# Attention pairs and sequence mixing on one core: another order of Q and K preparation, score groups, mixing steps and first loads

## The chip, the cores and the metric

The kernel runs on one NeuronCore of one Trainium2 chip. The metric is the time on the device for one execution, in microseconds (us), as the median of several runs. The engines are TensorE (PE for matmuls, PEld for its weight loads), VectorE (DVE), ScalarE (ACT), GpSimd (POOL) and SyncE (SP), which here only issues transfers.

## The reference

Three blocks follow one another: windowed attention, a block that mixes along the sequence and then through a wide layer (here called sequence mixing and the wide layer), and a gated layer at the end.

```python
# attention: B=2, H=8, S=768, D=64, n_global=8, n_local=96
scores = scale * np.matmul(q, k.transpose(0, 1, 3, 2))
keep = is_global | is_local               # rel >= 0 and rel < n_local, or column < n_global
scores = np.where(keep, scores + bias[None], -1000000000.0)
a = softmax(scores)                       # written out with max, exp and sum
x = np.matmul(a, v)                       # then heads are put side by side: (2, 768, 512)
# sequence mixing and wide layer
h = x.transpose(0, 2, 1) @ U @ V          # rank 32, along the sequence
u = x + h.transpose(0, 2, 1)
x = u + np.maximum(u @ w_ch1, 0.0) @ w_ch2    # 512 -> 2048 -> 512
# gated layer
xk = mu_k * x + (1.0 - mu_k) * x_prev;  xr = mu_r * x + (1.0 - mu_r) * x_prev
k = np.maximum(xk @ w_k, 0.0)
out = sigmoid(xr @ w_r) * (k * k @ w_v)
```

## The kernel before

The weight matrices come as 64-bit floats. The kernel loads their bits, turns them into 32-bit floats by integer and float operations (`conv`: names `stg`, `cvt`, `cvc`) and splits each into a high and a low part, so that a dense product is three matmuls.

**Attention** works on eight pairs of heads. Heads 2p and 2p+1 of one batch lie on partitions 0 to 63 and 64 to 127. Each pair is one call of `slot(pp)`, which emits four kinds of work: for the current pair the scores in three groups of two blocks of 128 rows (`score(pp, 0)`, `2`, `4`) and the division by the row sums (`norm`); for the next pair the transposes and copies of Q and K (`qprep`, `kprep`); for the pair before the transposes of the probabilities P (`trans`, six groups) and the product with V (`pv`); and the loads for pairs ahead (`load_qk(pp + 2)`, `load_v(pp)`).

In a score group TensorE writes two PSUM banks, VectorE adds the distances and reduces (line 301), ScalarE takes the exponential with a running sum (line 304), and GpSimd multiplies P by the inverse sums (line 315). `qprep` is six transposes on TensorE (line 261) and two copies on ScalarE (line 263); `kprep` is the same with lines 277 and 280, and then GpSimd copies K's first 32 columns beside each block (line 282). `trans` copies its bank to SBUF through `ecopy`, every third time on ScalarE (line 472), else on VectorE (line 474).

PSUM has eight banks in two rings of four: `"a"` for scores and the dense layers' first products, `"t"` for all transposes, for `pv`, for the mixing and for the dense layers' second products. A tile of a ring waits until the tile four places back has been read. P has ten buffers; q and k as loaded have one buffer each, v two.

**Side work** is woven into the slots by `weave`, which spreads the steps of several lists evenly: weight conversions (`CONV`), and from slot 5 on the sequence mixing of batch 0 (`u_steps(0)`, sixteen steps: six transposes `xtp`, the matmuls `gps` with U, the step `gs` that makes `uv` through ScalarE and VectorE, and eight matmuls `hps` with V with an addition to `yp` on VectorE, line 530), its split into high and low parts (`u_split`, lines 551 and 552, to `us`) and the first matmuls of the wide layer (`m_ch1`, `aps`). After the last slot the same mixing follows for batch 1 with `m_ch2` (`bps`, added to `yp` in line 592) between its steps. Then come the rest of the wide layer and the gated layer, dense matmuls to the end.

**Order.** The program text emits the steps; a planner of the framework then sets the order of each engine's queue, with the order of emission as priority and a plan of when buffers come free. Each engine runs its queue in order. So an instruction can run earlier than its place in the text: the two first loads of q for pair 1 are emitted before the loads of v for pair 0 and issued after most of them.

At the start `load_qk(0, "q")`, `limits()` (two loads on ScalarE's queue, three operations on VectorE), a few idle matmuls (`warm`) and `load_qk(0, "k")` are emitted first, then `qprep(0)`, `windows()` (the table of distances), `kprep(0)`, `load_qk(1)` and `load_v(0)`.

## Time and profile before

| what | value |
|---|---|
| median of 3 runs | 572.84 us |
| the three runs | 572.84, 572.85, 568.08 us |
| the profiled execution | 567.52 us |
| its span in the profile | 565.7 us |
| mean granted clock of TensorE | 0.985 |
| TensorE busy | 537.9 us, 95% of the span |

The profile is of one execution. Its span runs from the first instruction to the last; the time of the execution is a little longer. A busy share of TensorE is not a share of its peak, since matmuls overlap and their ends are modelled. The granted clock is a share of 2.4 GHz; the lower of its two levels is 1.2 GHz.

### The profile page before, as it was taken

The page shows a single profiled execution, that of the slowest core. Times are in us where ns is not written, and L with a number is a line of the kernel's source. Part 1 is how long each engine was busy: PE and PEld are TensorE (multiplying, and loading weights), DVE is VectorE, ACT ScalarE, POOL GpSimd, SP SyncE. Part 2 cuts the span into 40 slices and gives each one's busy share as a digit, 9 for nine tenths or more (in the row PEclk, how much of TensorE's full clock was granted, in tenths as well). Part 3 has the DMA queues.
Part 4 walks back from the last instruction along what each step waited for, and adds up shares of the span by engine and source line. Part 5 has one row for each costly group of instructions (what it writes and reads, how often), then busy time and mean ns, then how long its engine had stood idle before and what let it go on. Part 6 is the DMA issues. An engine that isn't in the chain of part 4 may idle for free.

```text
span 565.7 us, 7722 instructions
## 1 busy us (share of the span) xinstructions
PE 537.9 (95%) x2814; PEld 435.2 (77%) x2814; DVE 324.4 (57%) x703; ACT 230.4 (41%) x525; POOL 182.9 (32%) x223
## 2 busy tenths in 40 slices
PE   6898779899799999999999999999999999999996
PEld 3676657587588888888888888888788888888886
DVE  4657598998798726364282855579833442243101
ACT  3888678774445204032222242144361243124200
POOL 1555533770253104040120340254571244024200
PEclk9898899999899999999999999999999999999999
DMA  8865745444036402213040404004101000100011
GB/s 162 162 159 117 184 115 146 158 126 149 1 111 187 148 1 80 69 40 109 1 151 0 123 27 149 0 1 148 39 0 38 19 20 0 38 19 20 1 38 43
DMA packets 60206, 43.84 MB, mean 78 GB/s; under 512 B 51648, under 2 KB 51904, under 8 KB 60160
## 3 DMA queue, kind: packets, MB, share of 16 engines
q1 hardware_dynamic: 59872, 43.27, 27.2%
q8 instruction: 24, 0.39, 0.3%
q14 instruction: 22, 0.18, 0.1%
q10 hardware_dynamic: 288, 0.00, 0.0%
HBM read 40.11 MB, written 3.15 MB: 76 GB/s over the span
## 4 chain that ended last, share of the span: by engine, by line
PE 79%; DVE 8%; ACT 7%; POOL 2%; issue 2%; SPq 1%; DMA 1%; POOLq 0%; DVEq 0%; ACTq 0%
PE aps L575 23%; PE bps L588 20%; PE pvs L693 12%; PE kps L666 10%; PE prs L682 6%; ACT P L304 3%; PE s L294 2%; DVE cvc L423 2%; PE tp L329 2%; POOL P L315 2%; PE xb L342 1%; DVE cvc L425 1%; DVE P L301 1%; DMA qin<-in_q_dram 1%; PE hps L527 1%
## 5 line engine op out<-in xcount | busy, mean ns | idle before, releaser
L588 PE MATMUL bps<-rs,w2s 128*128 128x512 f32 x576 | 134.5, 393 | 0.5 <-DVE xt L474 0.3
L575 PE MATMUL aps<-us,w1s 128*128 128x512 f32 x576 | 133.9, 390 | 0.0
L588 PEld LDWEIGHTS bps<-rs,w2s 128*128 128x128 f32 x576 | 109.1, 190 | 23.7 <-DVE xt L474 0.5
L575 PEld LDWEIGHTS aps<-us,w1s 128*128 128x128 f32 x576 | 107.8, 188 | 22.5 <-issue 0.2
L578 ACT ACTIVATE rs<-aps 128x512 fp32r<-128x512 f32 x48 | 28.2, 593 | 102.8 <-PE aps L575 102.8
L666 PE MATMUL kps<-mix,wk 128*128 128x512 f32 x288 | 66.1, 389 | 1.2 <-DVE kf L671 1.2
L666 PEld LDWEIGHTS kps<-mix,wk 128*128 128x128 f32 x288 | 54.0, 188 | 12.8 <-DVE kf L671 1.6
L693 PE MATMUL pvs<-wv,kh 128*128 128x512 f32 (+1 forms) x208 | 61.8, 373 | 0.0
L579 DVE SCALAR_TENSOR_TENSOR rs<-aps,rs 128x512 fp32r<-128x512 f32 x48 | 32.8, 686 | 45.5 <-ACT rs L578 45.5
L315 POOL TENSOR_SCALAR P<-P,sm 128x256 f32<-128x256 f32 (+1 forms) x96 | 47.8, 518 | 28.9 <-DVE sm L311 10.6
L423 DVE SCALAR_TENSOR_TENSOR cvc<-cvc,cvt 128x512 uint32<-128x512 uint32 (+2 forms) x55 | 51.6, 940 | 9.7 <-ACT cvc L422 8.3
L422 ACT ACTIVATE cvc<-stg 128x512 f32<-128x512 f32 (+2 forms) x55 | 36.2, 665 | 44.9 <-DMA stg<-in_moe_w_ch_dram 18.2
L592 DVE TENSOR_TENSOR yp<-bps,yp 128x512 f32<-128x512 f32 (+1 forms) x64 | 33.9, 551 | 29.8 <-PE bps L588 29.8
L304 ACT ACTIVATE P<-P,nm 128x256 f32<-128x256 f32 (+1 forms) x96 | 46.2, 484 | 11.6 <-DVE nm L301 11.3
L432 POOL TENSOR_TENSOR w2s<-cvc,w2s 128x512 fp32r<-128x512 f32 x16 | 23.5, 1485 | 70.0 <-ACT w2s L430 70.0
L432 POOL TENSOR_TENSOR w1s<-cvc,w1s 128x512 fp32r<-128x512 f32 x16 | 23.6, 1492 | 69.2 <-ACT w1s L430 69.1
L648 POOL TENSOR_SCALAR mixt<-yp,mu 128x512 f32<-128x512 f32 (+1 forms) x32 | 21.6, 681 | 74.3 <-DVE mixf L650 29.8
L425 DVE SCALAR_TENSOR_TENSOR cvc<-stg,cvc 128x512 uint32<-128x512 uint32 (+1 forms) x54 | 44.8, 839 | 0.4
L693 PEld LDWEIGHTS pvs<-wv,kh 128*128 128x128 f32 x208 | 38.1, 188 | 6.9
L673 POOL TENSOR_TENSOR kl<-kf,kh 128x512 fp32r<-128x512 f32 x24 | 31.0, 1293 | 31.1 <-ACT kh L672 31.1
L301 DVE CUSTOM_DVE_ANT_0 P<-s,DW 128x256 f32<-128x256 f32 (+1 forms) x96 | 33.5, 395 | 10.8 <-PE s L294 10.7
L693 PE MATMUL pvs<-wv,kl 128*128 128x512 f32 (+1 forms) x104 | 38.8, 373 | 0.0
(104 smaller groups left out, 640.8 us busy)
## 6 DMA issues: line engine op xcount, KB each, us to landing
stg<-in_moe_w_ch_dram SPq DMA_DIRECT2D x32, 512.0 KB, 4.0
stg<-in_moe_w_k_dram SPq DMA_DIRECT2D x8, 512.0 KB, 3.7
stg<-in_moe_w_v_dram SPq DMA_DIRECT2D x8, 512.0 KB, 3.7
qin<-in_q_dram SPq DMA_DIRECT2D x16, 192.0 KB, 3.5
kin<-in_k_dram SPq DMA_DIRECT2D x16, 192.0 KB, 3.4
vin<-in_v_dram SPq DMA_DIRECT2D x16, 192.0 KB, 3.4
out_dram<-sg SPq DMA_DIRECT2D x11, 256.0 KB, 2.0
stg<-in_moe_w_r_dram SPq DMA_DIRECT2D x4, 512.0 KB, 3.8
```

Source lines behind the costliest of these rows:

```text
L301: nc.vector.tensor_tensor_reduce(out=P[:, t, 0:n], in0=sps[t][:, 256 * x:256 * x + n], in1=W, scale=2.0 ** -(2 * p + t + 1), scalar=TOP, o ...
L304: nc.scalar.activation(out=P[:, t, 0:n], in_=P[:, t, 0:n], func=ACTF.Exp, scale=-1.0, bias=z["nm"][:, i, t:t + 1], accum_out=z["sm"][:, i, ...
L315: nc.gpsimd.tensor_scalar(out=Pl, in0=Pl, scalar1=z["sm"][:, i, t:t + 1], scalar2=1.0, op0=ALU.mult, op1=ALU.mult)
L422: nc.scalar.activation(out=c.bitcast(F32), in_=Hh.bitcast(F32), func=ACTF.Copy, scale=2.0 ** -112)
L423: nc.vector.scalar_tensor_tensor(out=c, in0=c, scalar=3, in1=t, op0=ALU.logical_shift_left, op1=ALU.bitwise_or)
L425: nc.vector.scalar_tensor_tensor(out=c if plain is None else plain, in0=Hh, scalar=0x80000000, in1=c, op0=ALU.bitwise_and, op1=ALU.bitwise_or)
L432: nc.gpsimd.tensor_tensor(out=lo, in0=f, in1=hi.bitcast(F32), op=ALU.subtract)
L575: nc.tensor.matmul(ps, lhsT=wsl(("w1", g), lw, kk, f * 128, 128), rhs=us[c][:, lx, kk, :], start=(n == 0), stop=(n == 11))
L588: nc.tensor.matmul(ps, lhsT=wsl(("w2", g), lw, f, o * 128, 128), rhs=r[:, lx, f, :], start=(n == 0), stop=(n == 11))
L666: nc.tensor.matmul(ps, lhsT=wsl("wk", lw, kk, f * 128, 128), rhs=xk[:, lx, kk, :], start=(n == 0), stop=(n == 11))
L682: nc.tensor.matmul(pr, lhsT=xr[:, lx, kk, t * 128:(t + 1) * 128], rhs=wsl("wr", lw, kk, 0, 512), start=(n == 0), stop=(n == 11))
L693: nc.tensor.matmul(pv, lhsT=ks[c][lx][:, f, t * 128:(t + 1) * 128], rhs=wsl("wv", lw, f, c0, c1 - c0), start=(n == 0), stop=(n == 23))
```

## The change

- `slot`: `qprep` of the next pair is emitted first, then the score groups 0 and 2 in a row, then `kprep` and the loads of two pairs ahead; the transposes of the old P and the division follow.
- q as loaded gets two buffers instead of one.
- The start: `windows()` is a generator in two parts. The first part comes ahead of `limits()`; K of pair 0 is loaded through ScalarE's queue; the loads for pair 1 and v of pair 0 are emitted ahead of `qprep(0)`. Small tiles (`wz`, `nraw`, `nfl`) use buffers of P.
- Batch 0's mixing is emitted as its first eight steps in slot 5 and its last eight in slot 6, ahead of the split.
- Batch 1's mixing: first eight steps with one `m_ch2` among them, then the other three `m_ch2`, then the last eight steps, then the split by itself.

```diff
-        def limits():
-            nraw = const.tile([128, 2], I64, name="nraw")
-            nfl = const.tile([128, 2], F32, name="nfl")
+        def limits(scratch):
+            nraw = scratch(I64, 2, "nraw")
+            nfl = scratch(F32, 2, "nfl")
...
-            def load_qk(pp, names="qk"):
+            def load_qk(pp, names="qk", eng=nc.sync):
...
-                    z[nm] = in_p.tile([128, NT, 2, D], F32, tag=nm + "in", name=nm + "in")
+                    z[nm] = in_p.tile([128, NT, 2, D], F32, tag=nm + "in", name=nm + "in", bufs=2 if nm == "q" else 1)
                     for t in range(2):
-                        nc.sync.dma_start(out=z[nm][:, :, t, :],
+                        eng.dma_start(out=z[nm][:, :, t, :],
...
             load_qk(0, "q")
-            limits()
-            wz = ac.tile([128, 512], mybir.dt.bfloat16, name="wz")
+            wz = np_p.tile([128, 512], mybir.dt.bfloat16, tag="P", name="wz")
...
             warm(8)
-            load_qk(0, "k")
...
                 nc.vector.tensor_scalar(out=m0, in0=relf, scalar1=0.0, scalar2=None, op0=ALU.is_ge)
+                nc.gpsimd.memset(DW, BIG)
+                yield
                 nc.vector.tensor_scalar(out=m1, in0=relf, scalar1=nl, scalar2=None, op0=ALU.is_lt)
                 nc.vector.tensor_tensor(out=m0, in0=m0, in1=m1, op=ALU.mult)
-                nc.gpsimd.memset(DW, BIG)
...
                 add(cur and pp, load_v, pp)
+                add(nxt, qprep, pp + 1)
                 add(cur, score, pp, 0)
+                add(cur, score, pp, 2)
+                add(nxt, kprep, pp + 1)
+                add(pp + 2 < NPR, load_qk, pp + 2)
                 add(pre, trans, o, 0, 0)
                 add(pre, trans, o, 1, 0)
-                add(nxt, qprep, pp + 1)
-                add(cur, score, pp, 2)
                 add(cur, norm, pp, 0, 3)
                 add(pre, trans, o, 0, 1)
                 add(pre, trans, o, 1, 1)
-                add(nxt, kprep, pp + 1)
-                add(pp + 2 < NPR, load_qk, pp + 2)
                 add(cur, score, pp, 4)
...
+            wins = windows()
+            next(wins)
+            limits(lambda dt, n, nm: np_p.tile([128, 2], dt, tag="P", name=nm))
+            load_qk(0, "k", nc.scalar)
+            load_qk(1)
+            load_v(0)
             qprep(0)
+            next(wins)
             warm(3)
-            windows()
             kprep(0)
             warm(3)
-            load_qk(1)
-            load_v(0)
...
-                    side = {1: lambda: [A["constants"]], 5: lambda: u_steps(0), 6: lambda: st_split(0, slot_a),
+                    u0 = u_steps(0)
+                    side = {1: lambda: [A["constants"]], 5: lambda: u0[:8], 6: lambda: u0[8:] + st_split(0, slot_a),
...
-                weave(u_steps(1), st_ch2(0, 0)[:2])
+                u1, c0 = u_steps(1), st_ch2(0, 0)
+                weave(u1[:8], c0[:1])
+                weave(c0[1:])
+                weave(u1[8:])
...
-                weave(st_ch2(0, 0)[2:],
-                      [lambda kk=kk: u_split(1, kk, slot_d) for kk in range(4)])
+                weave(st_split(1, slot_d))
```

## Rows read from the trace of the kernel before

**Rows 1.** Page: busy time, share of the span and instructions by engine.

```profile
PE 537.9 (95%) x2814; PEld 435.2 (77%) x2814; DVE 324.4 (57%) x703; ACT 230.4 (41%) x525; POOL 182.9 (32%) x223
```

**Rows 2.** Busy time by stretch: slots 0 to 4, slots 5 to 7, mixing.

```profile
core 0: us, PE busy (x) PEld busy (x) DVE busy (x) ACT busy (x) POOL busy (x), PEclk, DMA share, GB/s
9.70:19.00 9.30, 6.19 (x42) 4.05 (x41) 4.50 (x26) 7.01 (x27) 2.61 (x7) 1.00 0.94 184
19.00:31.08 12.08, 11.58 (x100) 8.99 (x99) 7.34 (x35) 9.48 (x35) 6.67 (x17) 0.86 0.67 123
31.08:41.84 10.76, 10.34 (x104) 8.11 (x103) 7.27 (x33) 9.28 (x32) 5.47 (x14) 1.00 0.84 192
41.84:55.31 13.47, 11.52 (x104) 9.41 (x103) 9.66 (x39) 11.09 (x36) 7.34 (x16) 0.87 0.62 132
55.31:69.80 14.49, 11.64 (x109) 9.78 (x107) 8.02 (x34) 10.50 (x34) 8.70 (x18) 0.88 0.70 171
69.80:111.82 42.02, 36.21 (x273) 25.73 (x273) 38.02 (x112) 31.82 (x91) 20.81 (x31) 0.96 0.48 138
...
133.06:157.15 24.09, 20.00 (x98) 15.18 (x96) 17.87 (x33) 11.72 (x25) 4.60 (x4) 0.93 0.16 50
```

**Rows 3.** Waits of TensorE: total us, times, longest.

```profile
PE hps L527 <- DVE uv L522: 6.4, 2, 3.6
PE kps L277 <- ACT QS L263: 4.8, 2, 2.8
PE qps L261 <- DMA qin<-in_q_dram: 3.4, 2, 1.8
PE tp L329 <- POOL P L315: 2.3, 5, 0.5
```

**Rows 4.** Busy time of one stretch in slot 1, columns as in rows 2.

```profile
19.00:23.00 4.00, 4.00 (x21) 3.15 (x22) 2.63 (x12) 2.62 (x13) 1.14 (x4) 0.57 1.12 171
```

**Rows 5.** Timeline of the start: SyncE's issues and TensorE; start, duration, what.

```profile
1.84 1.89 SPq L177 DMA_DIRECT2D kin<-in_k_dram  x2
...
7.99 1.34 SPq L177 DMA_DIRECT2D qin<-in_q_dram  x2
...
8.28 0.85 PE L277 MATMUL kps<-ident,kin 128*128 128x128 f32 x6 [0.35 <-DMA kin<-in_k_dram]
...
13.28 0.85 PE L261 MATMUL qps<-ident,qin 128*128 128x128 f32 x6 [1.76 <-DMA qin<-in_q_dram]
```

**Rows 6.** Timeline of slot 3.

```profile
42.69 1.09 PE L329 MATMUL tp<-ident,P 128*128 128x128 f32 x8
43.72 2.21 PE L294 MATMUL s<-KK,QS 64*128 64x256 f32 x16
...
48.81 1.03 ACT L263 ACTIVATE QS<-qps,cs 128x512 f32<-128x512 f32 x2
...
49.53 1.30 PE L277 MATMUL kps<-ident,kin 128*128 128x128 f32 x6 [1.93 <-ACT QS L263]
```

**Rows 7.** Page: a group of instructions, and DMA issues of q.

```profile
L304 ACT ACTIVATE P<-P,nm 128x256 f32<-128x256 f32 (+1 forms) x96 | 46.2, 484 | 11.6 <-DVE nm L301 11.3
...
qin<-in_q_dram SPq DMA_DIRECT2D x16, 192.0 KB, 3.5
```

**Rows 8.** Timeline of batch 1's mixing, TensorE and VectorE.

```profile
144.69 0.71 PE L527 MATMUL hps<-uv 96*128 96x256 f32 x4 [3.63 <-DVE uv L522]
145.08 1.42 DVE L530 TENSOR_TENSOR yp<-hps,yp 128x256 f32<-128x256 f32 x4 [0.54 <-PE hps L527]
...
145.56 4.54 PE L588 MATMUL bps<-rs,w2s 128*128 128x512 f32 x12 [0.16 <-DVE yp L530]
146.42 1.42 DVE L552 TENSOR_TENSOR us<-yp,us 128x256 fp32r<-128x256 f32 x4
...
150.75 2.47 DVE L530 TENSOR_TENSOR yp<-hps,yp 128x512 f32<-128x512 f32 x4
...
151.69 5.62 PE L588 MATMUL bps<-rs,w2s 128*128 128x512 f32 x24
```

More of the change, by code (lines that the diff above doesn't have):

```diff
@@ L241, in windows @@
                 nc.vector.tensor_tensor(out=W0[:, 0:32], in0=W0[:, 0:32], in1=dg, op=ALU.min)
+                yield
             KS = 160
```

## Prediction

> **What bounds the kernel now.** I read the shares of the page first: TensorE is busy 95% of the span, no other engine over 57% [rows 1]. A kernel like this gains only where TensorE stands still or runs slowly, so the next view is the busy time by stretch, cut at the starts of the slots [rows 2], and then the list of what TensorE waited for [rows 3]. In rows 2 the reader should compare the first number (length) with PE, then look for the engine that is nearest to the length, then at the granted clock (PEclk, the last number but two).
>
> In the seven stretches shown TensorE is idle for 3.11 + 0.50 + 0.42 + 1.95 + 2.85 + 5.81 + 4.09 = 18.7 us, of 565.7 - 537.9 = 27.8 us in the whole span [rows 1, 2]. From 157.15 us on the program is dense matrix work; the diff touches nothing there, and I carry those 408.6 us over unchanged.
>
> There is a second loss. The granted clock is 0.86, 0.87, 0.88, 0.96 and 0.93 in five of the stretches. Between the full level (2.4 GHz) and the half level (1.2 GHz) a mean of 0.86 over 12.08 us means 2 x 0.14 x 12.08 = 3.4 us at the half level; the other four come out at 3.5, 3.5, 3.4 and 3.4 us. One of them is 0.57 over 4 us with TensorE busy throughout [rows 4]. Each follows a stretch with a wait or with thin work. Each costs about half of its 3.4 us, 1.7 us. So a wait that ends in such a drop costs itself and another 1.7 us, and the whole pot is 18.7 + 5 x 1.7 = 27 us. Slot 2, the third row of stretches [rows 2], is what a slot looks like without either: 10.34 us of TensorE in 10.76 us.
>
> Not all of the pot can be had, because the next engine is close. Of the two slots 3 and 4 (27.96 us) ScalarE (ACT) is busy 21.6; of slots 0 and 1 (21.38 us) 16.5; from 69.80 to 111.82 VectorE (DVE) is busy 38.0 of 42.0 us [rows 2]. What the other engine leaves free is the most that each stretch can gain.
>
> **The start and slots 0 and 1.** Now the loads of q for pair 1 are issued at 7.99, behind K and six loads of v on SyncE's queue, since the q buffer is single; TensorE waits 1.76 us for them at 13.28 [rows 5]. With two q buffers, and with K of pair 0 moved to ScalarE's queue, SyncE can issue them where K stood, at 1.84. They then land while pair 0 is still being prepared, and the 1.76 us go. In slot 1 the transposes of P no longer stand ahead of the scores, so the waits for GpSimd's (POOL's) division (at most 2.3 us: rows 3 sum five of them over all slots) are covered by six transposes of q, sixteen score matmuls and six transposes of k. With both gone, the drop of the clock in slot 1 (1.7 us) should go as well. That is up to 5.8 us; ScalarE allows 21.38 - 16.5 = 4.9. Against it: K of pair 0 now shares the transfer with q of pair 1, and TensorE already waits 0.35 us for K at 8.28 [rows 5]. A load of q or K is 0.39 MB; at the 184 GB/s of slot 0 [rows 2] 2.1 us. If all of it goes ahead of K, the first scores come 2.1 us later; if K is issued sooner than now, up to 0.4 us earlier. Between -4.9 and +2.1 I take **-2.5**, nearer the gain, because the q wait is removed outright and a later K shifts only this one point. ScalarE pays two issues; it is otherwise idle until its first copy, so nobody waits behind them. Splitting the window preparation (the two yields) moves the arithmetic that doesn't need the two limits ahead of the wait for them on VectorE. The sum takes nothing for it: the masks are needed only after K. If they became late, the first scores' reductions would be late by the same amount; the pieces moved are a few VectorE instructions, under 1 us.
>
> The Trainium skill, page "DMA: Bandwidth & Descriptors", section "Issuing engines are not separate DMA queues", says that starting transfers from a second engine saves only the issue time, since the same 16 DMA engines carry them. By it, moving K to ScalarE's queue by itself would be worth at most SyncE's 1.89 us for the two issues, and nothing where the transfers fill the engines; the DMA share of 0.94 in slot 0 agrees. The sum above counts nothing for that queue but the place it clears for q.
>
> **Slots 2 to 4.** Emitting both preparations first means that ScalarE copies Q before the exponentials. Slot 3 shows the opposite: sixteen score matmuls run in a row from 43.72, their exponentials fill ScalarE, the copy of Q runs only at 48.81, and the transposes of k wait 1.93 us for its bank [rows 6]. With the same wait in slot 4 (2.85) the pair is 4.8 us [rows 3], and two clock drops add 3.4: 8.2 us. ScalarE's free time in the two slots is 6.4 us; VectorE has more. Between 0 and -6.4 I take **-4**. Slot 2 has nothing to give.
>
> The copy of K's first block on GpSimd now stands ahead of this pair's division in its queue instead of behind it. That can only help the next slot. On SyncE, the loads of q and K for two pairs ahead stand earlier in the slot; K's waits for the transposes that free its buffer, and behind it only weight loads are queued. A load lands 3.5 us after its issue [rows 7], and it has most of a slot, so the transposes now at the head of the next slot find their data.
>
> **The new wait.** Only four banks serve transposes. In the new order q takes two, k two; the first transposes of the old P get q's banks back, but the second ones need k's, so they wait for ScalarE's copies of K. These stand behind the copies of Q (1.03) and up to eight exponentials at 0.484 us [rows 6, 7]: they start about 0.85 + 1.03 + 3.87 = 5.8 us into the slot. TensorE comes there after q (0.85), scores (2.21), k (0.85) and eight transposes of P (1.09): 5.0 us, or 6.1 if the third scores are put ahead [rows 5, 6]. Allowing 0.6 us for the first copy, the wait is between 0.3 and 1.4 us, in the six slots that have both. Since part of it is hidden when reductions start late anyway, the bounds are 0 and 1.4; I take 0.5: **+3.0** (0 to +8.4). Score buffers are no problem: six of the old P and four new are just the ten there are.
>
> **Slots 5 to 7.** The steps of the sequence mixing are split eight and eight over slots 5 and 6. The first of its second matmuls waited 2.8 us in slot 5 (with the 3.63 below, the 6.4 of rows 3), with a clock drop of 1.7. But VectorE leaves only 4.0 us free over the whole stretch, and the eight additions only move to slot 6, whose splits then come later for the matmuls of slot 7. Between -4.0 and +3.6 (the wait of 3.63 us in the same chain, moved there) I take **-1.5**.
>
> **From 133 to 157.** Now TensorE waits 3.63 us for the chain of small steps before the second mixing matmuls, and the twelve matmuls after it take 4.54 us at a low clock, where 24 take 5.62, that is 2.81 per twelve [rows 8]: a loss of 3.63 + 1.73 = 5.4 us. After the change 36 matmuls, 8.4 us, stand in that gap and cover it. But the second half, which hid the split of the next chunk, is used up. After the mixing matmuls (0.71 + 0.86 + 0.50) VectorE has additions of 1.42 and 2.47 us and then splits of 1.42 us [rows 8]. The first dense matmuls need the first split. If the splits run between the additions, it is there after 1.42 + 0.36 = 1.8 us, which the mixing matmuls hide; if after them, after 4.25 us, so TensorE waits 2.2 us, and with another drop 3.9. If the mixing matmuls are themselves held back by their banks, nothing of the 4.25 is hidden: 6.0 with a drop. So -5.4 to +0.6; I take **-3**, the middle of what the first two orders give.
>
> Sum: -2.5 - 4 + 3 - 1.5 - 3 = **-8 us**. The profiled execution took 567.52 (span 565.7 and 1.8 around it), so 559.5. The median of the timed runs is 572.84, 5.3 above it, the lowest 568.08. Counting from the median gives 564.8; I forecast the middle, **562**, since either level can come again. Taken together the bounds are wide (-20.7 to +14.7 around the profile), but not all ends come together.
>
> **Rivals.**
> - **The order is already so.** A planner, not the order of emission alone, sets each engine's queue: slot 3 already ran its second and third scores in a row [rows 6]. If it does much the same with the new text, only the start and the last part change. -2.5 - 3 gives 562 to 567.3, and less if the start is lost too. For it: the order differed from the text just where side work crowded the banks, which stays. Against: slots 1 and 2 follow the text. I put it at 565 to 570, **0.25**.
> - **The K copies become the bound (slower).** If ScalarE is still busy with the slot before, the second transposes wait as long as k's did in slot 3, 1.93 us, and the clock drops after each: 6 x (1.93 + 1.73) = 22 us, against gains of 11: +11, so **578**. It decides from a wait of about 1.1 us a slot with a drop (6 x 2.8 = 17, less 11, is +6, 573). For it: ScalarE is the fullest helper in slots 1 to 4. Against: the next scores can be put in the hole, and slot 2 runs full. **0.12**.
> - **The split is uncovered.** With the last part at its end of +0.6 in place of -3 the total is **566**. For it: VectorE's queue order decides, and the additions are emitted first. Against: the first kinds of work that are ready go first. **0.08**. The Trainium skill, "Perfetto Trace Analysis", section "Optimization Strategy", advises interleaving stretches whose fullest engine differs; by it this un-weaving of matmuls from splits is a loss, which is this rival. The trace of before agrees so far as the split lies beside dense matmuls there and costs no wait [rows 8].
>
> **How the numbers follow.** The forecast's own case has 0.55: 555 to 567. The rivals hold 0.45 between 564 and 580. The range 554 to 575 leaves out the far end of the slower rival and the best tenth. A measurement of this kernel tells about 1% (5.7 us) from no change. Faster by over 1%: 0.58 (the main case and part of the uncovered split); within 1%: 0.29; slower: 0.13.
>
> **What would show it.** In the profile after: no wait for q in slot 0, and slots 0 and 1 in about 19 us; no wait of k's transposes for Q, slots 3 and 4 in 24; no wait of the mixing matmuls after 133; the clock at 1.00 in more than two of the five stretches. Wrong would be: a wait of P's transposes for the copy of K in each slot; late first scores; a wait of the first dense matmuls for the split; or new low-clock stretches in place of the old.

## Result and the profile after

The changed kernel takes **564.22 us** (median of 15 runs, 562.27 to 565.74); the kernel before, timed beside it, 568.22 (15 runs, 566.14 to 573.14). The ratio is 0.9912, with a 95% interval of 0.9887 to 0.9937: faster by 0.9%, just short of the 1% that was to be told apart. The forecast was 562, the range 554 to 575. The profiled execution of the changed kernel took 565.74 us, its span is 563.7 us and its mean granted clock 0.985, as before. The runs of the kernel before fall into two levels, eleven from 566.14 to 568.59 and four from 571.18 to 573.14; those of the changed kernel lie at one.

Busy time by engine, which answers to [rows 1]:

```profile
PE 539.8 (96%) x2814; PEld 434.6 (77%) x2814; DVE 325.1 (58%) x703; ACT 229.8 (41%) x525; POOL 184.2 (33%) x223
```

The work is the same (2814 matmuls); what changed is where TensorE stands still. To see where, I cut both traces at four events that both have: the first product with V of pair 0, of pair 3 and of pair 7, and a run of 48 matmuls of the wide layer's second product (`bps`) after the mixing. From that run to the last addition of the output (`sg`) every kernel of this study takes 382.80 to 382.86 us, so all differences lie ahead of it or behind the last addition. Busy time by stretch of the kernel before (slots 2 to 4, slots 5 to 7, mixing of batch 1; columns as in [rows 2]):

```profile
27.67:66.46 38.79, 33.15 (x308) 26.87 (x307) 26.40 (x113) 32.38 (x110) 23.28 (x50) 0.92 0.65 147
66.46:130.51 64.05, 58.24 (x454) 43.52 (x453) 54.67 (x155) 46.46 (x129) 32.89 (x48) 0.97 0.51 143
130.51:178.23 47.72, 43.64 (x234) 35.02 (x233) 40.43 (x66) 22.45 (x44) 11.64 (x8) 0.96 0.32 100
```

The same three stretches of the changed kernel, columns as above:

```profile
27.82:62.86 35.04, 33.37 (x307) 25.50 (x306) 23.67 (x102) 29.33 (x98) 19.85 (x42) 1.00 0.70 152
62.86:127.19 64.33, 58.13 (x454) 42.80 (x453) 56.82 (x165) 47.88 (x137) 37.45 (x52) 0.97 0.56 146
127.19:173.47 46.28, 43.93 (x234) 35.11 (x233) 38.87 (x60) 21.06 (x42) 11.25 (x8) 0.96 0.28 85
```

The gain is in slots 2 to 4 (-3.75 us), a little in the mixing (-1.44); slots 5 to 7 lose 0.28 and the start 0.15 (27.67 to 27.82). That is -4.76. Of it the profiled execution kept only 1.78 (567.52 to 565.74), because the end behind the last addition took 2.7 us longer; the last part of this document comes to that. The waits of TensorE after, to be held against [rows 3] (total us, times, longest):

```profile
PE tp L329 <- POOL P L315: 3.4, 1, 3.4
PE s L294 <- DVE nm L301: 2.1, 2, 1.8
PE aps L579 <- DVE us L556: 1.9, 1, 1.9
...
PE tp L329 <- ACT QS L263: 1.2, 1, 1.2
...
PE xtp L508 <- ACT KK L280: 0.8, 1, 0.8
PE hps L531 <- DVE uv L526: 0.8, 1, 0.8
```

The two waits of k's transposes for Q (4.8 us) are gone, and of the two for `uv` (6.4) 0.8 is left. Three new ones stand on top: one group of P's transposes that waits for GpSimd, the scores that wait for the first reductions, and the first products of the wide layer (`aps`) that wait for the split.

**The start.** Timeline of the changed kernel, to be held against [rows 5]:

```profile
0.74 1.18 ACTq L177 DMA_DIRECT2D kin<-in_k_dram  x2
...
4.50 0.35 ACTq L52 DMA_DIRECT2D nraw<-in_n_global_dram  x1
6.03 0.35 ACTq L53 DMA_DIRECT2D nraw<-in_n_local_dram  x1
...
6.15 0.85 PE L261 MATMUL qps<-ident,qin 128*128 128x128 f32 x6 [1.57 <-DMA qin<-in_q_dram]
6.47 1.28 ACT L263 ACT_TABLE_LOAD   x1 [6.47 <-DMA qin<-in_q_dram]
...
7.48 0.82 PE L277 MATMUL kps<-ident,kin 128*128 128x128 f32 x6
...
9.15 0.82 PE L261 MATMUL qps<-ident,qin 128*128 128x128 f32 x6
...
9.90 1.79 PE L294 MATMUL s<-KK,QS 64*128 64x128 f32 x16
10.19 0.17 DVE L56 CAST nf<-nraw 128x2 f32<-128x2 int32 x1 [7.68 <-DMA nraw<-in_n_local_dram]
...
12.75 0.27 DVE L301 CUSTOM_DVE_ANT_0 P<-s,DW 128x128 f32<-128x128 f32 x1
...
13.52 1.23 PE L294 MATMUL s<-KK,QS 64*128 64x256 f32 x4 [1.83 <-DVE nm L301]
```

The kernel before had, on ScalarE and VectorE:

```profile
1.75 1.28 ACT L263 ACT_TABLE_LOAD   x1 [1.75 <-DVE cs L251]
...
10.69 0.29 DVE L301 CUSTOM_DVE_ANT_0 P<-s,DW 128x128 f32<-128x128 f32 x1 [1.88 <-PE s L294]
```

Pair 1's q is there in time: its transposes run at 9.15 without a wait, ahead of the scores (before: 13.28, after a wait of 1.76). But on ScalarE's queue the planner put the two small loads of the limits behind K, though the text emits them ahead of it, and they are issued only at 4.50 and 6.03 us. K is not what they wait for: its two issues end at 1.92. In the trace each of the two small issues waits for a semaphore that one of pair 0's two loads of q counts on as well, and those land at 4.47 and 6.01. VectorE waits 7.68 us for them, the table of distances is late, and so the first reduction (L301) runs at 12.75, though the scores began at 9.90. TensorE fills the four banks of the scores (sixteen matmuls) and waits 1.83 us. ScalarE's own work is late as well: the load of its function table (`ACT_TABLE_LOAD`) runs at 6.47 us, behind the second of these issues, and the first copy of Q behind it at 7.77.

**Slot 7.** Timeline of TensorE, VectorE and GpSimd:

```profile
101.07 0.48 POOL L315 TENSOR_SCALAR P<-P,sm 128x256 f32<-128x256 f32 x1 [2.57 <-DVE sm L311]
101.51 1.70 POOL L436 TENSOR_TENSOR w2s<-cvc,w2s 128x512 fp32r<-128x512 f32 x1
...
102.01 1.75 DVE L556 TENSOR_TENSOR us<-yp,us 128x512 fp32r<-128x512 f32 x1
103.20 4.20 POOL L315 TENSOR_SCALAR P<-P,sm 128x256 f32<-128x256 f32 x5
...
106.08 0.88 PE L329 MATMUL tp<-ident,P 128*128 128x128 f32 x5 [3.35 <-POOL P L315]
...
107.69 4.11 PE L579 MATMUL aps<-us,w1s 128*128 128x512 f32 x12
```

GpSimd's division of P (L315) comes late: it waits 2.57 us for the sums from VectorE, is then held up by a weight conversion of 1.70, and runs its last five blocks while VectorE makes the splits of batch 0. The first two of the five take 1.43 and 1.42 us beside VectorE's splits and conversions, where a block mostly takes 0.48. TensorE stands for 3.35 us; the twelve products behind it take 4.11 us (before, 24 took 5.62: [rows 8]), with the clock at its half level.

**The mixing of batch 1.** TensorE and VectorE, to be held against [rows 8]:

```profile
137.12 8.47 PE L592 MATMUL bps<-rs,w2s 128*128 128x512 f32 x36
...
145.43 0.52 PE L531 MATMUL hps<-uv 96*128 96x256 f32 x3
146.24 3.80 DVE L534 TENSOR_TENSOR yp<-hps,yp 128x256 f32<-128x256 f32 x8
149.95 7.56 DVE L556 TENSOR_TENSOR us<-yp,us 128x256 fp32r<-128x256 f32 x8
150.87 7.35 PE L579 MATMUL aps<-us,w1s 128*128 128x512 f32 x24 [1.93 <-DVE us L556]
```

The 36 products of the second layer cover the chain that TensorE waited 3.63 us for. But VectorE makes all eight additions first (3.80 us) and only then the splits, and with no product left to run TensorE waits 1.93 us for the first of them, with the clock at its half level behind it (151 to 155 us).

### The profile page after: what moved, and what is told of

The parts are those of the page before. It is cut to its first block, busy times and chain, and to the rows that moved or that the text cites. A ratio compares the mean times of both kernels' runs of the same rounds, so it can differ in the third digit from the quotient of the medians.

```text
span 563.7 us, 7717 instructions
## 1 busy us (share of the span) xinstructions
PE 539.8 (96%) x2814; PEld 434.6 (77%) x2814; DVE 325.1 (58%) x703; ACT 229.8 (41%) x525; POOL 184.2 (33%) x223
## 4 chain that ended last, share of the span: by engine, by line
PE 81%; DVE 8%; ACT 5%; DMA 2%; POOL 1%; issue 1%; SPq 0%; POOLq 0%; ACTq 0%; DVEq 0%
PE aps L579 24%; PE bps L592 19%; PE pvs L701 12%; PE kps L674 10%; PE prs L690 6%; ACT P L304 3%; PE s L294 3%; PE tp L329 2%; PE xb L342 2%; DVE cvc L427 2%; DVE cvc L429 1%; DVE yp L534 1%; PE xtp L508 1%; DMA qin<-in_q_dram 1%; PE gps L517 1%
## 5 line engine op out<-in xcount | busy, mean ns | idle before, releaser
L579 PE MATMUL aps<-us,w1s 128*128 128x512 f32 x576 | 136.7, 396 | 1.9 <-DVE us L556 1.9
L592 PE MATMUL bps<-rs,w2s 128*128 128x512 f32 x576 | 132.8, 389 | 0.0
L579 PEld LDWEIGHTS aps<-us,w1s 128*128 128x128 f32 x576 | 109.8, 191 | 25.6 <-DVE us L556 2.4
L315 POOL TENSOR_SCALAR P<-P,sm 128x256 f32<-128x256 f32 (+1 forms) x96 | 50.4, 546 | 26.0 <-DVE sm L311 13.7
L436 POOL TENSOR_TENSOR w1s<-cvc,w1s 128x512 fp32r<-128x512 f32 x16 | 22.4, 1423 | 63.0 <-ACT w1s L434 63.0
L301 DVE CUSTOM_DVE_ANT_0 P<-s,DW 128x256 f32<-128x256 f32 (+1 forms) x96 | 33.3, 392 | 9.1 <-PE s L294 9.0
```

The lines of the kernel that those rows point to most:

```text
L315: nc.gpsimd.tensor_scalar(out=Pl, in0=Pl, scalar1=z["sm"][:, i, t:t + 1], scalar2=1.0, op0=ALU.mult, op1=ALU.mult)
L436: nc.gpsimd.tensor_tensor(out=lo, in0=f, in1=hi.bitcast(F32), op=ALU.subtract)
L579: nc.tensor.matmul(ps, lhsT=wsl(("w1", g), lw, kk, f * 128, 128), rhs=us[c][:, lx, kk, :], start=(n == 0), stop=(n == 11))
L592: nc.tensor.matmul(ps, lhsT=wsl(("w2", g), lw, f, o * 128, 128), rhs=r[:, lx, f, :], start=(n == 0), stop=(n == 11))
```

## Experiments

Each kernel was compared with the kernel before in runs of its own. The table has the median of all its runs, the ratio with its interval, and from the profiled execution of each the time of pair 0's first product with V, the lengths of the three stretches, and the end (span less the start of the last addition), all in us. The rows of before and after are those of the fences above.

| kernel | median | ratio | pair 0 | slots 2-4 | slots 5-7 | mixing | end |
|---|---|---|---|---|---|---|---|
| before | 568.22 | | 27.67 | 38.79 | 64.05 | 47.72 | 4.65 |
| after | 564.22 | 0.9912 (0.9887-0.9937) | 27.82 | 35.04 | 64.33 | 46.28 | 7.38 |
| E1 limits first | 564.25 | 0.9916 (0.9885-0.9947) | 27.14 | 35.21 | 65.45 | 46.32 | 6.43 |
| E2 slot order only | 570.94 | 1.0057 (1.0016-1.0097) | 30.07 | 35.55 | 65.02 | 50.54 | 6.79 |
| E3 mixing 1 only | 566.67 | 0.9968 (0.9921-1.0016) | 26.59 | 38.70 | 64.08 | 46.72 | 4.58 |
| E4 mixing 0 back | 563.87 | 0.9931 (0.9904-0.9958) | 26.35 | 35.03 | 63.50 | 46.69 | 6.52 |
| E5 K ahead of q | 566.46 | 0.9943 (0.9908-0.9979) | 27.37 | 35.70 | 66.52 | 46.28 | 6.33 |
| E6 scores first | 565.06 | 0.9943 (0.9914-0.9971) | 28.46 | 35.37 | 65.31 | 46.28 | 6.44 |
| E7 one block kept | 560.17 | 0.9843 (0.9798-0.9887) | 26.24 | 35.04 | 64.49 | 42.45 | 6.94 |
| E8 start only | 570.72 | 0.9993 (0.9953-1.0033) | 28.11 | 36.24 | 69.45 | 47.51 | 4.63 |
| E9 E7 and E4 | 560.46 | 0.9841 (0.9802-0.9879) | 26.40 | 35.03 | 65.39 | 43.76 | 6.29 |
| E10 slot and start | 564.89 | 0.9925 (0.9892-0.9957) | 26.29 | 35.03 | 63.33 | 47.37 | 6.45 |
| E11 before, one block kept | 563.48 | 0.9881 (0.9839-0.9923) | 28.09 | 38.85 | 64.06 | 42.83 | 4.77 |
| E12 E7 shifted | 558.42 | 0.9858 (0.9831-0.9884) | 26.10 | 35.50 | 65.27 | 42.44 | 4.57 |

**E1: the limits' loads first.** The changed kernel with `limits` emitted ahead of the windows and K.

```diff
+            limits(lambda dt, n, nm: np_p.tile([128, 2], dt, tag="P", name=nm))
             wins = windows()
             next(wins)
-            limits(lambda dt, n, nm: np_p.tile([128, 2], dt, tag="P", name=nm))
             load_qk(0, "k", nc.scalar)
```

> The changed kernel, with the two small loads of the limits emitted ahead of the loads of K, so that they are issued at the start and not at 4.5 and 6.0 us. Theory (masks late): the first reduction moves from 12.75 us back to about 10.7, the wait of TensorE for it (1.83 us) goes, and the kernel gains 2 to 4 us on the changed one (ratio to before 0.982 to 0.988). Rival (slots 0 and 1 are bound by ScalarE or by q anyway): the masks are early but the fourth pair's products start where they did, and the ratio stays at 0.991.

Its timeline at the start:

```profile
2.41 0.55 ACTq L177 DMA_DIRECT2D kin<-in_k_dram  x1
...
5.92 1.51 PE L261 MATMUL qps<-ident,qin 128*128 128x128 f32 x6 [1.13 <-DMA qin<-in_q_dram]
...
7.30 0.17 DVE L56 CAST nf<-nraw 128x2 f32<-128x2 int32 x1 [5.31 <-DMA nraw<-in_n_local_dram]
...
8.97 1.04 PE L277 MATMUL kps<-ident,kin 128*128 128x128 f32 x6 [0.26 <-DMA vin<-in_v_dram]
...
11.24 2.91 PE L294 MATMUL s<-KK,QS 64*128 64x128 f32 x20
12.20 0.29 DVE L301 CUSTOM_DVE_ANT_0 P<-s,DW 128x128 f32<-128x128 f32 x1 [1.58 <-PE s L294]
```

The limits land 2.9 us sooner (7.30 against 10.19). But K's transposes run at 8.97 instead of 7.48, the scores at 11.24 instead of 9.90, and now the reductions wait for the scores. The first reduction gains 0.55 us, the time nothing. That the masks alone hold the start falls. Why K's transposes are later is not shown: the planner put the second half of K behind the limits, but TensorE waits only 0.26 us there. The work ahead of them ran slower, q's transposes 1.51 us instead of 0.85 and the idle matmuls 1.49 instead of 0.81, and E4, E7, E9 and E10, whose loads of K stand as in the changed kernel, begin them at 8.45 to 8.79.

**E2: the slot order alone.** The kernel before with only the reordered calls in `slot`; one q buffer, old start, old mixing.

```diff
+                add(nxt, qprep, pp + 1)
                 add(cur, score, pp, 0)
+                add(cur, score, pp, 2)
+                add(nxt, kprep, pp + 1)
+                add(pp + 2 < NPR, load_qk, pp + 2)
                 add(pre, trans, o, 0, 0)
```

> The kernel before with the new order of the slot alone (single q buffer, old start, old mixing). Theory (the slot order is what gains in slots 2 to 4, about 3.7 us up to the product of pair 3): ratio 0.992 to 0.995, that product starts 3 us or more earlier than 66.46. Rival (the second q buffer or the start carries it): no gain, ratio 0.998 to 1.003, and waits for q.

Slots 2 to 4 gain 3.24 us, most of what the whole change gains there. But the kernel is slower: in slot 0 the transposes of pair 1's q run at 13.33 after the same wait of 1.78 us as before, and pair 0's first product with V comes 2.4 us later (30.07), with the clock at the half level for most of 15 to 25 us. The mixing, whose text is unchanged, takes 50.54 with two low stretches. So the order by itself gains nothing in the whole time; together with the new start and its second q buffer it does (E10). Its runs spread from 567.73 to 575.93 us and the profiled one took 572.87, so other runs may lose less to the clock.

**E3: batch 1's mixing alone.** The kernel before with only the new order of the mixing after the last slot (the four `weave` lines of the diff).

> The kernel before with the new order of batch 1's mixing alone. Theory (the covered wait of 3.63 us and its clock drop are replaced by a wait for the split of about 1.9 us with a drop): gain 1 to 2 us, ratio 0.996 to 0.998. Rival (both losses go): 5 us, 0.991. Other rival (nothing): 1.000.

The mixing takes 46.72, 1.00 less than before; batch 1's wait for `uv` is gone and the wait of `aps` for the split, 1.9 us, has come. The ratio cannot be told from 1.

**E4: batch 0's mixing back in one slot.** The changed kernel with its sixteen steps in slot 5 again.

```diff
-    5: lambda: u0[:8], 6: lambda: u0[8:] + st_split(0, slot_a),
+    5: lambda: u0, 6: lambda: st_split(0, slot_a),
```

> The changed kernel with batch 0's mixing put back into slot 5 as a whole and the split alone in slot 6. Theory (the move into slot 6 makes the splits late and causes the wait of 3.35 us for the division at 106 with its clock drop): that wait goes, and the kernel is as fast or up to 3 us faster than the changed one, ratio 0.986 to 0.991. Rival (the move gains its 2.8 us wait and the late wait has another cause): slower than the changed one by 2 to 4 us, ratio 0.995 to 0.998.

The wait of 3.35 us in slot 7 is not there any more, but the scores wait 2.41 us for VectorE's reductions at 80.14 instead. Slots 5 to 7 take 63.50 instead of 64.33; E9 and E10, with the same text there, take 65.39 and 63.33, so these 0.8 us are not shown to belong to the edit. In the whole time it can't be seen.

**E5 and E6: another start.** E5: limits first, and K through SyncE again, ahead of pair 1's q. E6: the same, and in slot 0 the scores ahead of pair 1's q.

```diff
+            limits(lambda dt, n, nm: np_p.tile([128, 2], dt, tag="P", name=nm))
+            load_qk(0, "k")
             wins = windows()
             next(wins)
-            limits(lambda dt, n, nm: np_p.tile([128, 2], dt, tag="P", name=nm))
-            load_qk(0, "k", nc.scalar)
...
-                add(nxt, qprep, pp + 1)
+                add(nxt and pp, qprep, pp + 1)
                 add(cur, score, pp, 0)
                 add(cur, score, pp, 2)
+                add(nxt and not pp, qprep, pp + 1)
```

> The changed kernel with the old start's order of transfers: limits first on ScalarE's queue, K of pair 0 on SyncE's queue ahead of q of pair 1 (two q buffers kept). Theory (K shares the transfer with q of pair 1, so either the masks or the first scores are late): masks and K on time, first reduction at about 10.7 to 11 us, product of pair 0 from 27.8 to 25 or 26, ratio 0.982 to 0.988. Rival (in the new slot order q of pair 1 is now what the first scores wait for, since its transposes stand ahead of them): TensorE waits for q until 11 or 12, ratio 0.991 or above.

> As the run before it, and in slot 0 alone the scores stand ahead of the preparation of q for pair 1. Theory (nothing in slot 0 needs q of pair 1 first): product of pair 0 at 25 us or earlier, ratio 0.980 to 0.987. Rival (ScalarE's work bounds slots 0 and 1 whatever comes first): within 0.5 us of the run before it.

In E5 the limits land at 5.51 us, but the transposes of pair 1's q, which stand ahead of the first scores, run only at 10.83, and the scores at 11.69. They wait for no load: K's transposes and the idle matmuls ahead of them took 1.51 and 1.49 us (0.82 and 0.81 in the changed kernel), with the granted clock at 0.50 from 9 to 11 us. E6 takes q out of the way, and the first reduction runs at 11.68 instead of 12.65; pair 0 is no sooner for it (28.46). Neither is faster than the changed kernel.

**E7: one block of products kept for the split.** The changed kernel, but the last of the four `m_ch2` is woven with the split instead of standing ahead of the second half of the mixing.

```diff
                 weave(u1[:8], c0[:1])
-                weave(c0[1:])
+                weave(c0[1:3])
                 weave(u1[8:])
...
-                weave(st_split(1, slot_d))
+                weave(st_split(1, slot_d), c0[3:])
```

> The changed kernel with one of the three blocks of dense matmuls (12 matmuls, 2.7 us) kept back beside the split of batch 1. Theory (the wait of 1.93 us for the split and its clock drop of 1.7 are what the mixing gave back): the wait goes, the other two blocks (5.4 us) still cover the chain, gain 2 to 3.5 us on the changed kernel, ratio 0.985 to 0.988. Rival (the additions of the kept block delay the split, or the clock drop belongs to something else): ratio 0.991.

Timeline of its mixing, TensorE and VectorE:

```profile
135.70 5.75 PE L592 MATMUL bps<-rs,w2s 128*128 128x512 f32 x24
...
141.29 0.52 PE L531 MATMUL hps<-uv 96*128 96x256 f32 x3
...
142.10 3.80 DVE L534 TENSOR_TENSOR yp<-hps,yp 128x256 f32<-128x256 f32 x8
...
144.64 2.89 PE L592 MATMUL bps<-rs,w2s 128*128 128x512 f32 x12
...
145.81 3.01 DVE L556 TENSOR_TENSOR us<-yp,us 128x256 fp32r<-128x256 f32 x4
...
147.36 10.82 PE L579 MATMUL aps<-us,w1s 128*128 128x512 f32 x47
```

24 products are enough to cover the chain to `uv` (done at 140.2), and the twelve kept ones (2.89 us) cover the additions, so `aps` runs on without a wait. The stretch at 1.00 of the clock:

```profile
125.77:168.22 42.45, 42.02 (x234) 34.04 (x233) 36.80 (x57) 20.18 (x40) 11.68 (x8) 1.00 0.28 87
```

Against the changed kernel's 46.28 that is 3.83 less: 1.93 for the wait, and 43.93 - 42.02 = 1.91 of TensorE's busy time, the price of the drop behind it. The kernel is faster than both: its slowest run, 561.10, lies under the changed kernel's fastest, 562.27.

**E8: the start alone.** The kernel before with the new start and the second q buffer.

> The kernel before with the new start and the second q buffer alone (old slot order, old mixings). Theory (the new start gains nothing by itself, since the 1.76 us wait for q is exchanged for late masks or late K; it only pays for what the new slot order loses at the start): ratio 0.997 to 1.003, product of pair 0 between 27 and 29 us. Rival (the start is what gains): ratio 0.992 to 0.995.

No gain that the ratio shows: pair 0 at 28.11, with the clock at half from 16 to 22 us. Two things came unasked: slots 2 to 4 gained 2.55 us (38.79 to 36.24) without the new order, and slots 5 to 7 lost 5.4, with the clock at half from 84 to 97 us. But five of its twelve runs took 565.03 to 566.58 us and seven 570.67 to 571.33; the profile is of one of the seven, so the loss in slots 5 to 7 need not be in the others.

**E9: E7 with batch 0's mixing back.** Both edits above.

> The changed kernel with one block of the wide layer's second product kept beside the split of batch 1, and with batch 0's mixing whole in slot 5 again. Theory (slot 7's wait of 3.35 us at 106.08 comes from the second half of batch 0's mixing in slot 6, and the drop behind it from the wait): it goes, and the time falls by 1 to 3 us below the version with one block kept: 557 to 559 us, ratio 0.977 to 0.983. Rival (what slot 7 gains slot 5 loses to its wait for the step uv, as undoing it by itself showed no measurable difference): 560 to 561 us, ratio 0.983 to 0.987. The third matmul stretch from the last pair to the second products should stay at 42 to 43 us in both.

The rival held: 560.46, as E7. What slot 7 might gain doesn't show; the mixing at 43.76 has a wait of 1.1 us that E7 doesn't have.

**E10: slot order and start, both mixings as before.**

```diff
-                u1, c0 = u_steps(1), st_ch2(0, 0)
-                weave(u1[:8], c0[:1])
-                weave(c0[1:])
-                weave(u1[8:])
+                weave(u_steps(1), st_ch2(0, 0)[:2])
...
-                weave(st_split(1, slot_d))
+                weave(st_ch2(0, 0)[2:],
+                      [lambda kk=kk: u_split(1, kk, slot_d) for kk in range(4)])
```

> The changed kernel with both mixings as before: only the slot's new order, the start and the second q buffer. Theory (the slot order gives 3.5 us in slots 2 to 4, but needs the second q buffer so as not to lose 2.4 us in slots 0 and 1): 564.5 to 566 us, ratio 0.993 to 0.997, and from the last pair to the second products 47 to 49 us, as before. Rival (the mixing segment slows down with the new slot order as it did with that order alone, 50.5 us): 567 to 569 us, ratio 0.998 to 1.002.

As the theory had it: 564.89, with the mixing at 47.37. Nearly the whole gain of the change is here; its two edits of the mixing together are worth nothing that the medians (564.22, 564.89) can tell.

**E11: the kernel before with one block kept.** E3 with E7's edit.

> The kernel before with nothing changed but batch 1's mixing: its second products in a row, with one of the four blocks kept for the split. Theory (both losses in the mixing go, the wait for uv and the wait for the split, and the mixing is independent of the slots): the stretch from the last pair to the second products falls from 47.7 to 42.5 us, and the time to 563 to 564 us, ratio 0.991 to 0.994. Rival (part of what the version with one block kept gained was a luckier clock, or needs the new slots): 565 to 567 us, ratio 0.995 to 0.999.

The mixing falls to 42.83 (-4.89) and the time to 563.48, ratio 0.9881, with everything ahead of it within 0.5 us of the kernel before. So this one edit gives by itself as much as the whole change, and it adds to the slots' gain (E7).

**E12: the same work, shifted queues.** E7 with twelve small VectorE instructions and eight small matmuls more at the start.

```diff
             nc.vector.memset(wz, 0.0)
+            for _ in range(12):
+                nc.vector.memset(wz[:, 0:16], 0.0)
...
+                for _ in range(8 if n == 8 else 0):
+                    nc.tensor.matmul(wps[:, 0:64], lhsT=wz[:, 0:128], rhs=wz[:, 0:64], start=True, stop=True)
```

> The version with one block kept beside the split, with twelve more small instructions on VectorE and eight more small matmuls (with their weight loads) on TensorE at the start, where both engines wait for the first loads anyway: the work behind them is the same, only its place in each engine's stream of instructions moves. It asks about the end: the kernels with the new slot order run on for 6.3 to 7.4 us after the last addition of the output (SyncE waits 1.9 to 2.8 us for TensorE's or VectorE's queue in the closing instructions), those with the old slot order for 4.6 to 4.8. Theory (the closing wait depends on the place in the stream, so that any shift may move it): it goes, the end takes 4.6 to 4.8 us, and the time falls to 558 us, ratio 0.980. Rival (it belongs to the slot order whatever the place): the end still takes 6.3 to 7.4 us, 560 us, ratio 0.984. A wait that stays does not refute the theory, since this shift may be too small.

The end takes 4.57 us again and the median is 558.42, the lowest of the study. The ratio is 0.9858 and not the 0.980 of the theory, no better than E7's, as the kernel before took 566.62 in that comparison and 568.37 in E7's. That the end is shorter is read from the trace; that the kernel is faster for it is not shown.

## Why the prediction was right, and where not

**Direction and size.** The sum said -8 us; the medians show -4.0, the stretches -4.76. The direction was right and the size twice too large. That the forecast of 562 is only 2.2 us off is in part luck: it counted from the middle between two levels, about 570; the kernel before came out at 568.22 beside the changed one, near its profile and not near the 572.84 that was shown, and 568.22 - 8 would have been 560.2. Of the chances, "faster by over 1%" had 0.58 and "within 1%", which the 0.9% is, 0.29. Two of the signs of being wrong came: a wait of the first dense matmuls for the split, and new low-clock stretches. Ahead of the dense part the kernel before had five of 3.4 us; the changed kernel's profile has three, at about 14.5 to 21.3, 106.6 to 110.1 and 151.0 to 154.4 us.

**The start: -2.5 was too much; the sign is likely right.** Five kernels have the very same start (after, E4, E7, E9, E10): pair 0 at 27.82, 26.35, 26.24, 26.40, 26.29. Three have the old one with the old slots (before, E3, E11): 27.67, 26.59, 28.09. By the middle ones, 26.35 and 27.67, that is -1.3, with a spread as large; the profiled run of the changed kernel is the one that got nothing, with the clock at half from 14.5 to 21.3 us, where the other four have the full level. The 1.76 us of q went, as said. Two steps failed. One is that ScalarE "pays two issues" and "nobody waits behind them": it also issues the two loads of the limits, which wait for q to land, and its table load, done at 3.03 before, starts only at 6.47. The other is "the sum takes nothing" for the masks: the first reduction ran at 12.31 to 12.75 us in the five, at 10.69, 12.03 and 11.71 in the three. How much of the gain each of them cost is not shown. E1, E5 and E6 bring the limits early, and pair 0 is no sooner than in the four (27.14, 27.37, 28.46); but they move other loads or matmuls too, and TensorE's speed at the start differs from profile to profile. As for K on ScalarE's queue, which the Trainium skill ("DMA: Bandwidth & Descriptors", "Issuing engines are not separate DMA queues") says saves only the issue: the trace agrees that there is little to have, since its transposes waited 0.35 us for K before, at 8.28, and for nothing after, at 7.48 (at 8.55 in E7, with the same new start).

**Slots 2 to 4: -4 held, its account did not.** The waits for Q went; the stretch is 3.75 us shorter, 1.2 us of the new wait below included. TensorE's idle time there fell from 38.79 - 33.15 = 5.64 to 35.04 - 33.37 = 1.67, so the whole gain is idle time. The granted clock rose from 0.92 to 1.00 and yet busy time did not fall. By tile, the 3.4 us that I counted for two drops came back nearly whole: k's transposes (`kps`) fell from 3.66 to 2.57 us, those of P (`tp`) from 10.55 to 9.04 and the first products with V (`xa`) from 3.06 to 2.63. But the scores (`s`) rose from 9.26 to 12.47. Many of them now stand in small pieces between the transposes, which is the likeliest reason. In slot 2 before, and in slot 3 after:

```profile
36.35 1.13 PE L294 MATMUL s<-KK,QS 64*128 64x256 f32 x8
```

```profile
46.89 0.70 PE L294 MATMUL s<-KK,QS 64*128 64x256 f32 x2
```

Two score matmuls by themselves take 0.70 us, eight in a row 1.13; the prediction had no term for that. Nor was the order alone the cause: E2 (order) and E8 (new start with the second q buffer) each give most of it, -3.24 and -2.55, and both together -3.75.

**The K-copy wait: +3.0, measured 2.0.** It came in two slots instead of six, 1.2 us in slot 4 and 0.8 in slot 5 (put down to the copies of Q and of K). In slots 2 and 3 the planner set the third scores in pieces of two between the groups of P's transposes, as the prediction had it ("the next scores can be put in the hole"): that hides the wait, at the price of the longer scores just named. The slower rival needed 1.1 us in each slot and a drop behind it; it did not happen.

**Slots 5 to 7: -1.5, measured +0.28.** The wait for `uv` in slot 5 fell from 2.8 to 0.8 us. The reason was wrong: E4, E9 and E10 have batch 0's mixing whole in slot 5 and no such wait at all, and E2, with the slot order alone, lacks it too, so the order took it and not the split over two slots. The bound of +3.6 named the new wait, but in the wrong place: not the products wait for the later splits, but P's transposes, for GpSimd, which gets VectorE's sums late and then runs slowly beside its splits. What the split over two slots costs in all is below what one profile shows (E4).

**The mixing: -3, measured -1.44** (-1.00 by E3, -1.09 by E10 against the changed kernel). Here the mechanism was right and the choice wrong. The prediction had two orders: splits between the additions, or after them with a wait of 2.2 and a drop, 3.9 in all. The second came true (1.93 and 1.91), and 5.4 - 3.9 = 1.5 is what it gives; I had taken the middle. "The first kinds of work that are ready go first" was the wrong argument: VectorE ran all eight additions, which are emitted first, ahead of the first split, and did so in E7 too. What the third rival describes thus happened, at -1.44 and not at the +0.6 that its 566 counts. E7 and E11 show that the loss is no part of the edit's purpose: one of four blocks held back removes it. The Trainium skill's advice ("Perfetto Trace Analysis", "Optimization Strategy") to interleave stretches whose fullest engine differs agrees with E7: 46.28 to 42.45.

**"Carried over unchanged".** True for the dense part to 0.06 us, false for the end, which the prediction had no term for.

## What to carry to other kernels

When work is pulled forward to cover one chain, look what it had been covering: keep back just enough of it for the next chain (here 24 products for one, 12 for the other, -4.9 us). When a load is moved to another engine's queue, list what that queue already carries and what each issue waits for: here two small loads waited for the landing of a large one, and the engine's own first work came late behind them. And compare a change stretch by stretch between events that both traces have: the whole time mixes the gain with the clock's and the end's own changes.

## What the hardware showed that I had not expected

**The end took two lengths.** In the nine kernels with the new slot order ahead of E12, the span ends 6.29 to 7.38 us after the last addition begins, in the four with the old order 4.58 to 4.77. SyncE's own waits, in the closing lines, of before, after, E10 and E12 (total us, times, longest):

```profile
SPq L754 <- PEq L754: 0.6, 2, 0.5
```

```profile
SPq L761 <- PEq L761: 2.8, 2, 2.6
```

```profile
SPq L759 <- DVEq L759: 2.1, 1, 2.1
```

```profile
SPq L765 <- PEq L765: 0.6, 2, 0.5
```

SyncE waits some 2 us for TensorE's or VectorE's queue, and a few small instructions more at the start of the program, for which pair 0 is no later (26.10), take that wait away (E12: 4.57). So in its profile some 2 us of the change's gain went into this wait. That it hangs on where the instructions lie in the stream rests on this one shift; what the queue waits for there no view shows.

**A 1 KB load that waits for a large one.** The limits' loads landed 10.2 us into the run where they were issued behind K, and at 5.5 where they were issued first (E2, E5). The issue was what came late: 4.50 and 6.03 us against 0.74 and 1.20 in E2. In all seven kernels with the changed kernel's order of first loads (after, E4, E7 to E10, E12) each of the two issues shares its semaphore with a load of pair 0's q and comes within 0.03 us of that load's landing; in E1 and in those that issue the limits first it waits for no semaphore.

**The clock's low stretches move between like programs.** E9 and E10 have the same text up to the mixing; between 82 and 92 us the one has the half level throughout, the other mostly the full one:

```profile
82.00:92.00 10.00, 9.65 (x52) 7.31 (x52) 8.70 (x19) 6.72 (x13) 4.77 (x7) 0.50 0.19 54
```

```profile
82.00:92.00 10.00, 9.60 (x80) 7.42 (x78) 9.91 (x27) 7.90 (x15) 5.97 (x8) 0.88 0.21 62
```

TensorE is as busy in both, and does 52 matmuls in the one and 80 in the other. Slots 5 to 7 differ by 2.06 us (65.39, 63.33). The start of after and E7, with the same text up to the mixing, is such a pair too (27.82, 26.24):

```profile
14.00:22.00 8.00, 7.79 (x37) 5.59 (x36) 4.42 (x28) 7.49 (x30) 2.80 (x7) 0.57 0.95 179
```

```profile
14.00:22.00 8.00, 6.44 (x48) 4.55 (x47) 5.25 (x34) 8.00 (x32) 4.01 (x10) 1.00 1.00 200
```

One profile can therefore not size a term of 1 or 2 us; the stretches in which several kernels agree (35.03 to 35.04 for slots 2 to 4, five times) can.
